# Chunk-selected attention and a gated MLP on one core: kmax left in PSUM until kmin is subtracted, with all queues reordered

## The chip, the cores and the metric

One Trainium2 chip, one NeuronCore. The time is device microseconds of a whole execution, the median of several runs; lower is better. One execution was also recorded by the hardware profiler, and all rows below come from it. TensorE is called PE there, VectorE DVE, ScalarE ACT, GpSimd POOL; SP is the engine that only issues DMAs here.

## The reference

Four batches of eight heads, 768 positions, head dimension 64. Keys come in chunks of 32. For every query and chunk an upper bound of the score is formed from the chunk's smallest and largest key per dimension; the six chunks with the highest bound are attended to. The result feeds a gated MLP block with a matrix multiply over positions.

```python
k_chunks = k.reshape(B, H, nc, 32, D)
k_min, k_max = k_chunks.min(axis=3), k_chunks.max(axis=3)
ub = sum_d maximum(q * k_min, q * k_max)          # [B, H, S, 24 chunks]
top = argsort(where(causal, ub, -1e9))[..., -6:]
scores = where(chunk of the key in top and causal, q @ k.T / 8, -1e9)
x = softmax(scores) @ v                            # laid out as [B, S, 512]
h = gelu(x @ w_in); u, v = split(h); v = layernorm(v) * g_ln
out = x + (u * (w_sg @ v + b_sg)) @ w_out
```

## The kernel before

The 32 heads are 16 pairs (p = 0 to 15), four to a batch. The upper bound is computed as q @ kmin + relu(q) @ (kmax - kmin), so that two small matmuls (`ub`) give it. The tile `W` holds kmin (its row 0) and kmax - kmin (its row 1) of a pair, 24 chunks each.

The program is a list of operations, each a function of an engine with what it reads and writes. `TABLE` holds the written-out order of each engine's queue as numbers of operations in that list, then the PSUM slot of every tile, and the engine of the operations that may run on one of several. Waits follow from reads and writes; an operation on a PSUM tile (`ps=`) also waits for every earlier operation of another engine on that tile, and the slot comes free when all of its operations are done. Engines work through their queues strictly in order. Operations are named here by tag:

- `kn`, `qn`, `vn`, `wi`, `ws`, `wo`: loads, issued by SP. `kT`, `dt_x`: DMA transposes. `st`: stores.
- `ktr`, `qtr` (TensorE, line 549): transposes of a pair's k and q, in halves hf of 384 columns, into PSUM.
- `kmm` (VectorE, line 579), pairs 0 to 7 (`kside`): minimum (m = 0) and maximum (m = 1) of the 12 chunks of one half, both from PSUM into `W` in SBUF. `wsub` (line 591): one subtraction per pair over 24 chunks, `W` row 1 minus row 0, all in SBUF, after all four `kmm`.
- `kev`, `qev`: evictions of the transposed halves to SBUF. `rel`: relu(q). `qcast`, `kcast`, `vcast`: casts to bf16.
- pairs 8 to 15: `kred` (line 598) reduces k as loaded, `perm` (line 620, `bounds`) puts the results in place by matmuls for two pairs at a time, in two tiles R; `wcp` (line 628) copies kmin and kmax of one tile to `W`, and `wsub` (line 633) subtracts 48 chunks of both pairs in SBUF, after both copies.
- `ub` (TensorE, lines 682 and 729), then `utr`, `m8`, `dn`, `dt` on VectorE select the chunks; `qd` puts the mask rows where the scores' matmuls read them; `mrow` fills the constant mask rows.
- `sc` (lines 838, 844 and 798) scores, `exp` (lines 853 and 804) on ScalarE, `aff` the causal cut on GpSimd, `pv` and `pvd` (lines 876, 883) the product with v, `rcp` and `xs` the division.
- the MLP of a batch: `hv`, `hu` (lines 930, 970) with `gv`, `gu` (gelu) on ScalarE; `bns`, `bna`, `var`, `rstd`, `nmr`, `vhat` the layer norm; `pt` (line 987), `vs`, `gt`, `ou` (line 1010), `os` (line 1016), `st`. `wic`, `wsc`, `woc`, `wst`, `wev` prepare the weights, `bev` the bias.

A batch's MLP runs between the attention of the next batch's pairs; the last batch's MLP has nothing beside it.

Of the kernel before, what the change touches and what calls it, by code (L numbers as in the profile page):

```python
# [1231 lines left out]
```

## Time and profile before

| | us |
|---|---|
| median of 3 runs (209.26 to 210.39) | 210.3 |
| the profiled execution | 211.3 |
| its span, first to last instruction | 209.6 |
| PE busy | 198.8 (95%) |
| DVE busy | 180.5 (86%) |
| ACT busy | 161.4 (77%) |
| POOL busy | 121.9 (58%) |

The busy time of PE holds pipelined matmuls whose ends are modelled, so it says where PE stood, not how near it is to its peak. A row of a timeline may stand for several instructions in sequence (x4); "idle before" is how long the engine had stood, and what ended it.

### The profile page before, as it was taken

Reading aid. Unit: us, or ns where it says so; the run is one execution under the profiler, and the core shown is the slowest. Engines: PE = TensorE matmul, PEld = TensorE weight load, DVE = VectorE, ACT = ScalarE, POOL = GpSimd, SP = SyncE. Lnnn points to the kernel's source line nnn. Section 1 sums busy time; section 2 is a strip of 40 time slices with the busy share of each in tenths; the row PEclk is TensorE's granted clock in tenths of the full one; section 3 lists DMA queues with packets and bytes.
Section 4 is the critical chain, followed back from the end, with each engine's and each line's share of the span. In section 5 each row is a group of like instructions: output and inputs, shape, how many; then the busy total and the mean of one; then the engine's idle time right before and its main releaser. Section 6 shows DMA issues by size and latency. Waiting matters only on the chain.

```text
span 209.6 us, 6043 instructions
## 1 busy us (share of the span) xinstructions
PE 198.8 (95%) x2392; PEld 129.0 (62%) x2392; DVE 180.5 (86%) x527; ACT 161.4 (77%) x238; POOL 121.9 (58%) x170
## 2 busy tenths in 40 slices
PE   5799999999999999999999999999899999899993
PEld 1655777755566677785456667677346767355652
DVE  3699899989999999999999899967868857587994
ACT  2559999997999899899788989888678887366000
POOL 8636799989579959958735957266580531002000
PEclk9999999999999999999999999999999999999999
DMA  6999999979949999999998995679968052401207
GB/s 143 221 252 208 227 243 316 298 206 276 222 126 255 238 146 252 192 182 153 218 218 154 217 206 125 133 146 117 200 122 191 4 91 42 149 0 50 100 32 272
DMA packets 103006, 36.38 MB, mean 174 GB/s; under 512 B 97729, under 2 KB 98497, under 8 KB 102978
## 3 DMA queue, kind: packets, MB, share of 16 engines
q1 hardware_dynamic: 102978, 36.00, 82.8%
q8 instruction: 19, 0.31, 0.7%
q14 instruction: 9, 0.07, 0.1%
HBM read 24.38 MB, written 6.29 MB: 146 GB/s over the span
## 4 chain that ended last, share of the span: by engine, by line
PE 61%; DVE 15%; ACT 8%; DMA 6%; SPq 3%; issue 3%; POOL 2%; DVEq 0%
PE PSG L987 11%; PE PSC L798 8%; PE PSG L970 8%; PE PSG L930 7%; PE PSG L1010 6%; PE PSG L876 5%; PE PSG L549 5%; ACT E L853 4%; PE PSG L729 3%; DMA vn<-in_v_dram 2%; DVE stats L939 2%; PE PSC L838 2%; DMA out_dram<-osb 2%; DVE osb L1016 2%; PE PSG L682 2%
## 5 line engine op out<-in xcount | busy, mean ns | idle before, releaser
L804 ACT ACTIVATE E<-PSC 128x1024 bf16<-128x1024 f32 (+1 forms) x72 | 62.6, 915 | 6.5 <-PE PSC L798 5.6
L798 PE MATMUL PSC<-QA,KA 128*128 128x128 bf16 (+2 forms) x336 | 37.6, 246 | 0.4 <-ACT E L804 0.4
L987 PE MATMUL PSG<-wsgT,vhat 128*128 128x384 bf16 x192 | 35.0, 326 | 0.0
L809 POOL TENSOR_SCALAR_AFFINE_SELECT E<-E 128x768 bf16<-128x768 bf16 x24 | 20.5, 863 | 24.0 <-ACT E L804 23.4
L798 PEld LDWEIGHTS PSC<-QA,KA 128*128 128x128 bf16 x336 | 24.2, 98 | 11.1 <-ACT E L804 3.8
L368 POOL CAST QA<-qT 64x768 bf16<-64x768 f32 (+1 forms) x27 | 22.2, 821 | 6.9 <-DVE qT L368 5.2
L975 ACT ACTIVATE uT<-PSG 128x384 bf16<-128x384 f32 x32 | 15.4, 486 | 12.1 <-PE PSG L970 11.8
L987 PEld LDWEIGHTS PSG<-wsgT,vhat 128*128 128x128 bf16 x192 | 17.9, 98 | 10.7 <-ACT vhat L953 0.4
L970 PE MATMUL PSG<-xT,winb 128*128 128x384 bf16 x128 | 23.8, 327 | 0.2 <-DVE U L738 0.2
L930 PE MATMUL PSG<-winb,xT 128*128 128x512 bf16 x96 | 22.2, 379 | 1.7 <-DVE PSG L993 0.9
L1010 PE MATMUL PSG<-woutb,uT 128*128 128x512 bf16 (+1 forms) x108 | 23.7, 355 | 0.0
L934 ACT ACTIVATE vgb<-PSG 128x512 f32<-128x512 f32 x24 | 14.3, 597 | 10.3 <-PE PSG L930 10.1
L993 DVE SCALAR_TENSOR_TENSOR PSG<-PSG,glnT,bsgbc 128x384 f32<-128x384 f32 x32 | 19.6, 614 | 2.9 <-PE PSG L987 2.4
L853 ACT ACTIVATE E<-PSC 128x1024 bf16<-128x1024 f32 (+1 forms) x24 | 20.6, 931 | 1.8 <-PE PSC L844 1.8
L368 POOL COPY QA<-Dt 32x576 bf16<-32x576 bf16 x20 | 13.8, 688 | 11.7 <-DVE Dt L757 10.6
L876 PE MATMUL PSG<-vx,E 128*128 128x65 bf16 x480 | 19.8, 194 | 0.4 <-ACT E L804 0.2
L579 DVE TENSOR_REDUCE Wall<-PSG 128x12 f32<-128x384 f32 x32 | 16.6, 543 | 3.4 <-PE PSG L549 3.4
L939 DVE BATCH_NORM_STATS2 stats<-vgb 128x6 f32<-128x512 f32 x24 | 16.1, 683 | 3.6 <-ACT vgb L934 3.3
L876 PEld LDWEIGHTS PSG<-vx,E 128*128 128x128 bf16 x480 | 17.1, 98 | 2.6 <-issue 0.6
L970 PEld LDWEIGHTS PSG<-xT,winb 128*128 128x128 bf16 x128 | 11.3, 98 | 11.2 <-ACT uT L975 3.0
L899 DVE TENSOR_TENSOR XS<-PSG,rden 128x384 bf16<-128x384 f32 x32 | 17.6, 551 | 0.7
L997 DVE TENSOR_TENSOR uT<-PSG,uT 128x384 bf16<-128x384 f32 x32 | 17.4, 550 | 0.6
(115 smaller groups left out, 377.0 us busy)
## 6 DMA issues: line engine op xcount, KB each, us to landing
vn<-in_v_dram SPq DMA_DIRECT2D x16, 384.0 KB, 5.5
qn<-in_q_dram SPq DMA_DIRECT2D x30, 192.0 KB, 4.5
out_dram<-osb SPq DMA_DIRECT2D x21, 256.0 KB, 2.5
kn<-in_k_dram SPq DMA_DIRECT2D x8, 384.0 KB, 6.3
kn<-in_k_dram SPq DMA_DIRECT2D x14, 192.0 KB, 4.6
uT<-in_moe_w_sg_dram SPq DMA_DIRECT2D x4, 384.0 KB, 5.4
vgb<-in_moe_w_in_dram SPq DMA_DIRECT2D x3, 512.0 KB, 7.5
vhat<-in_moe_w_sg_dram SPq DMA_DIRECT2D x2, 384.0 KB, 6.6
```

Of the source, the lines that this page charges most:

```text
L368: return e.tensor_copy(dst(), src())
L798: r = e.matmul(t.ap()[:, o:o + n], KA[w][i][:, 128 * kb:128 * kb + 128], QA[w][i][:, q0:q0 + n], start=True, stop=True)
L804: P.op("act", lambda e, t=t, c0=c0, c1=c1, i=i: e.activation(E[es][:, i, c0:c1], t.ap()[:, 0:c1 - c0], ACTF.Exp, scale=SCALE), act(c1 - c0 ...
L809: P.op("pool", lambda g, ev=ev: g.affine_select(ev, ev, pattern=[[0, NT], [1, 128]], compare_op=ALU.is_ge, fill=0.0, base=0, channel_multi ...
L853: P.op("act", lambda e, t=t, c0=c0, c1=c1, n=n: e.activation(E[es][:, :, c0:c1], t.ap().rearrange("p (i x) -> p i x", i=2)[:, :, 0:n], ACT ...
L876: r = e.matmul(t.ap()[:, 65 * qb:65 * qb + 65], E[es][:, i, a:a + 128], vx[w][:, kb, i, :], start=first, stop=False, skip_group_check=True)
L930: r = e.matmul(t.ap()[:, 0:F], xT[s][:, dk, 128 * qt:128 * qt + 128], winb[:, dk, F:DFF], start=(dk == 0), stop=(dk == NDK - 1))
L939: P.op("dve", lambda d, qt=qt, st=st: d.bn_stats(stats[st][:], vg[qt]), dve(F, 60), ("bns", b, qt), reads=[("vg", qt)], writes=[("stats", ...
L970: r = e.matmul(t.ap()[:, 0:TG], winb[:, dk, 128 * fb:128 * fb + 128], xT[s][:, dk, TG * tg:TG * tg + TG], start=(dk == 0), stop=(dk == NDK ...
L987: r = e.matmul(t.ap()[:, 0:TG], vhat[s][:, sb, 128 * fb:128 * fb + 128], wsgT[:, sb, TG * tg:TG * tg + TG], start=(sb == 0), stop=(sb == N ...
L993: P.op("dve", lambda d, t=t, fb=fb, tg=tg: d.scalar_tensor_tensor(t.ap()[:, 0:TG], t.ap()[:, 0:TG], glnT[:, fb:fb + 1], bsgbc[:, TG * tg:T ...
L1010: r = e.matmul(t.ap()[:, 0:c1 - c0], gT[s][:, fb, 128 * qt:128 * qt + 128], woutb[:, fb, c0:c1], start=(fb == 0), stop=(fb == NF - 1))
```

## The change

For pairs 0 to 7 the maximum of a half now goes to spare columns (384 to 395) of the PSUM tile that it was read from, and each half has a subtraction of its own right behind, 12 chunks wide, that reads kmax from PSUM and kmin from `W` and writes `W` row 1. For pairs 8 to 15 each tile R has a copy of kmin alone and a subtraction that reads kmax from PSUM. [...]

```diff
             c0, c1 = cols(hf, run)
+            n0, n1 = c0 // 32, c1 // 32
             for m, op in ((0, ALU.min), (1, ALU.max)):
-                P.op("dve", lambda d, m=m, op=op, t=t, c0=c0, c1=c1: d.tensor_reduce(
-                    W[w][:, m, c0 // 32:c1 // 32], t.ap()[:, 0:c1 - c0].rearrange("p (c x) -> p c x", x=32) if run == 0 else
...
-                    dve(c1 - c0), ("kmm", p, hf, m), reads=[t, ("W0", w)], writes=[("W", w, m, hf)], ps=[t])
+                P.op("dve", lambda d, m=m, op=op, t=t, c0=c0, c1=c1, n0=n0, n1=n1: d.tensor_reduce(
+                    W[w][:, 0, n0:n1] if m == 0 else t.ap()[:, TG:TG + n1 - n0],
+                    t.ap()[:, 0:c1 - c0].rearrange("p (c x) -> p c x", x=32), axis=AX.X, op=op),
+                    dve(c1 - c0), ("kmm", p, hf, m), reads=[t, ("W0", w)],
+                    writes=[("W", w, 0, hf) if m == 0 else ("Wm", w, hf)], ps=[t])
+            P.op("dve", lambda d, t=t, n0=n0, n1=n1: d.tensor_tensor(
+                W[w][:, 1, n0:n1], t.ap()[:, TG:TG + n1 - n0], W[w][:, 0, n0:n1], op=ALU.subtract), dve(12), ("wsub", p, hf),
+                reads=[("W", w, 0, hf), ("Wm", w, hf)], writes=[("W", w, 1, hf)], ps=[t])
...
-        ws = [("W", w, m, hf) for m in range(2) for hf in range(2)]
-        P.op("dve", lambda d: d.tensor_tensor(W[w][:, 1, 0:NC], W[w][:, 1, 0:NC], W[w][:, 0, 0:NC],
-                                              op=ALU.subtract), dve(24), ("wsub", p), port=True, reads=ws, writes=ws)
...
+        wv = lambda R, m: Wall[:, w0:w0 + 2, m, 0:NC].rearrange("p x (t R r) -> p x t R r", R=2, r=2)[:, :, :, R, :]
         for R in range(2):
-            P.op("dve", lambda d, R=R: d.tensor_copy(
-                Wall[:, w0:w0 + 2, :, 0:NC].rearrange("p x m (t R r) -> p (x m) t R r", R=2, r=2)[:, :, :, R, :], view(R)),
...
-        P.op("dve", lambda d: d.tensor_tensor(Wall[:, w0:w0 + 2, 1, 0:NC], Wall[:, w0:w0 + 2, 1, 0:NC],
-                                              Wall[:, w0:w0 + 2, 0, 0:NC], op=ALU.subtract), (125, 208),
-             ("wsub", pairs[0]), port=True, reads=ws, writes=ws)
+            P.op("dve", lambda d, R=R: d.tensor_copy(wv(R, 0), view(R)[:, 0::2]), dve(24),
+                 ("wcp", pairs[0], R), reads=[ts[R]] + [("W0", p % NW) for p in pairs],
+                 writes=[("W", p % NW, 0, R) for p in pairs], ps=[ts[R]])
+            P.op("dve", lambda d, R=R: d.tensor_tensor(wv(R, 1), view(R)[:, 1::2], wv(R, 0), op=ALU.subtract), dve(24),
+                 ("wsub", pairs[0], R), reads=[ts[R]] + [("W", p % NW, 0, R) for p in pairs],
+                 writes=[("W", p % NW, 1, R) for p in pairs], ps=[ts[R]])
```

All queues, all PSUM slots and the engine of some sixty operations are written anew in `TABLE`. The numbers in it shift, since there are 1304 operations where there were 1292. Read back into names, the stretches that matter below are:

```
VectorE, start   before  kmm_0_1_0 kev_0_1 kmm_0_1_1 . qev_0_0 qev_1_0 kmm_0_0_0 kmm_0_0_1 wsub_0 kmm_1_0_1 kmm_1_0_0 kmm_1_1_0 kmm_1_1_1 utr_0_0 wsub_1 m8_0_0
                 after   qev_1_1 qev_0_1 kmm_0_0_1 kmm_0_0_0 kmm_0_1_1 kmm_0_1_0 wsub_0_0 wsub_0_1 kmm_1_1_1 kmm_1_1_0 kmm_1_0_0 wsub_1_1 kmm_1_0_1 utr_0_0 wsub_1_0 m8_0_0
VectorE, 43 us   before  wev_0 qev_5_0 wsub_5 bns_0_1 wsub_4 rel_5 bns_0_0 bna_0_1 bns_0_3 bna_0_0 bna_0_3 utr_4_1
                 after   wev_0 bns_0_1 qev_6_1 bns_0_0 bna_0_1 bns_0_3 utr_4_1     (wsub_4_0 to wsub_5_0 stand earlier)
VectorE, 80 us   before  kred_11_0 wcp_8_0 os_0_1 wcp_8_1 rcp_5_0 kred_11_1 wsub_8 xs_5_0
                 after   wcp_8_1 wcp_8_0 gt_0_1_1 kred_11_0 os_0_2 os_0_1 wsub_8_0 wsub_8_1 kred_11_1 rcp_5_0
VectorE, end     before  os_3_2 os_3_0 os_3_3_256 os_3_3_0 os_3_1 and four halves
                 after   os_3_0 os_3_3_256 os_3_5_256 os_3_2 os_3_1 and four halves
SP, start        before  qn_1_0 kn_0_1_1 qn_1_1 kn_0_0_1 qn_0_0_0 qn_0_1_0 kn_0_0_0 kn_0_1_0 kn_1_0 qn_0_1_1 qn_0_0_1 kn_1_1
                 after   qn_1_1 kn_0_1_0 qn_1_0 qn_0_1_1 kn_0_1_1 qn_0_0_1 qn_0_0_0 kn_0_0_1 kn_0_0_0 qn_0_1_0 kn_1_1 kn_1_0
SP, weights      before  vn_2 wi_3 vn_3 wi_2 qn_5_0 wi_1 wi_0 ws_0 ws_2
                 after   vn_2 ws_0 qn_5_0 vn_3 wi_0 wi_2 wi_1 wi_3 qn_6_1 qn_6_0 ws_2
SP, 110 us       before  kT_11_0 kT_11_1 qn_15_1 kT_12_1 kn_15 vn_11 qn_15_0 vn_9 st_0_5 vn_10
                 after   kT_10_1 qn_15_1 vn_8 vn_9 kn_14 vn_10 kn_15 qn_15_0 kT_11_0
```

Operations that change engine: from VectorE to ScalarE kev_0_1, kev_4_0_0, kev_4_1_1, qev_0_0, qev_1_0, qev_2_1, qev_3_0, qev_4_1, qev_5_0, qev_12_1, qev_14_1, rel_5, wev_5, xs_4_1 (six instructions there), vhat_0_5, vhat_2_3, vhat_3_1, vhat_3_4; from ScalarE to VectorE qev_0_1, qev_1_1, qev_3_1, qev_6_1, qev_11_1, qev_12_0, kev_2_0, kev_3_1, kev_5_0_0, xev_0_0, both bev, vhat_3_2, vhat_3_5; from GpSimd to ScalarE qcast_0, qcast_1, wic_1, mrow_3_0_0, kcast_8_1, kcast_10_0, both kcast_12, kcast_15_0, woc_0, woc_3, qd_7_0, qd_9_1, qd_11_0, rel_8, vcast_11; from ScalarE to GpSimd ini_0, rel_1, rel_3, rel_7, rel_10, wsc_0, wsc_4, both qd_6, qd_12_0, kcast_10_1, kcast_11_1, kcast_14_1, vcast_7, vcast_9, vcast_12, vcast_15, qcast_13_0.

## Rows read from the trace of the kernel before

**Rows 1.** Stretches: length, then busy us (instructions) of PE, PEld, DVE, ACT, POOL; clock, DMA.

```profile
15.00:39.00 24.00, 23.58 (x461) 17.39 (x461) 22.53 (x81) 23.15 (x32) 19.86 (x25) 1.00 1.09 257
39.00:62.40 23.40, 22.92 (x224) 14.47 (x221) 22.14 (x67) 21.89 (x40) 18.83 (x26) 1.00 0.90 214
62.40:98.50 36.10, 35.79 (x555) 25.63 (x553) 35.15 (x104) 33.85 (x50) 29.45 (x41) 1.00 1.17 205
...
112.00:130.00 18.00, 17.48 (x286) 12.15 (x285) 16.46 (x41) 16.39 (x22) 14.71 (x19) 1.00 1.05 184
130.00:148.00 18.00, 17.12 (x262) 12.30 (x261) 14.90 (x59) 16.02 (x19) 9.70 (x14) 1.00 0.80 137
148.00:180.00 32.00, 31.07 (x311) 18.66 (x311) 24.13 (x57) 23.60 (x33) 11.54 (x16) 1.00 0.53 118
```

**Rows 2.** Lines 591, 633 and 628: count, duration ns min/median/max, first and last start.

```profile
L591 DVE TENSOR_TENSOR Wall<-Wall x8: 138/194/717, 10.4 to 64.5; 128x24 f32<-128x24 f32 x8
L633 DVE TENSOR_TENSOR Wall<-Wall x4: 172/198/778, 83.0 to 130.4; 128x48 f32<-128x48 f32 x4
L628 DVE COPY Wall<-PSG x8: 169/200/210, 81.2 to 125.7; 128x48 f32<-128x48 f32 x8
```

**Rows 3.** Timeline at two subtractions: start us, us, engine, line; idle before.

```profile
45.02 0.83 POOL L368 COPY KA<-INDF 64x768 bf16<-64x768 bf16 x1
45.16 0.72 DVE L591 TENSOR_TENSOR Wall<-Wall 128x24 f32<-128x24 f32 x1
82.91 0.82 POOL L368 CAST QA<-qT 64x768 bf16<-64x768 f32 x1
83.02 0.78 DVE L633 TENSOR_TENSOR Wall<-Wall 128x48 f32<-128x48 f32 x1
83.85 0.72 PE L729 MATMUL PSG<-qT,Wall 64*32 64x288 f32 x16 [0.31 <-DVE Wall L633]
```

**Rows 4.** Groups by line and shape on VectorE: busy us, mean ns; idle before.

```profile
L579 DVE TENSOR_REDUCE Wall<-PSG 128x12 f32<-128x384 f32 x32 | 16.6, 543 | 3.4 <-PE PSG L549 3.4
L993 DVE SCALAR_TENSOR_TENSOR PSG<-PSG,glnT,bsgbc 128x384 f32<-128x384 f32 x32 | 19.6, 614 | 2.9 <-PE PSG L987 2.4
L997 DVE TENSOR_TENSOR uT<-PSG,uT 128x384 bf16<-128x384 f32 x32 | 17.4, 550 | 0.6
```

**Rows 5.** Groups by line and shape on ScalarE and GpSimd.

```profile
L365 ACT ACTIVATE qT<-PSG 128x384 f32<-128x384 f32 x23 | 11.0, 496 | 2.3 <-PE PSG L549 2.1
L365 ACT ACTIVATE rT<-qT 128x576 f32<-128x576 f32 x9 | 6.0, 681 | 0.1
L365 ACT ACTIVATE vx<-vn 128x768 bf16<-128x768 f32 x5 | 4.2, 847 | 0.8 <-DMA vn<-in_v_dram 0.8
L423 ACT ACTIVATE CMw<-CMw 64x32 bf16<-64x32 bf16 x1 | 0.2, 228 | 3.4 <-POOL CMw L416 3.4
L367 POOL TENSOR_SCALAR rT<-qT 128x576 f32<-128x576 f32 x5 | 8.2, 1650 | 0.8 <-ACT qT L365 0.7
```

**Rows 6.** Timeline of ScalarE and TensorE near 123 us.

```profile
122.64 0.85 ACT L365 ACTIVATE vx<-vn 128x768 bf16<-128x768 f32 x1 [0.78 <-DMA vn<-in_v_dram]
124.46 0.62 PE L798 MATMUL PSC<-QA,KA 128*128 128x128 bf16 x7 [0.36 <-ACT E L804]
```

**Rows 7.** Timeline of VectorE at the start.

```profile
10.75 1.95 DVE L579 TENSOR_REDUCE Wall<-PSG 128x12 f32<-128x384 f32 x4 [0.17 <-PE PSG L549]
```

**Rows 8.** Chain of waits (first row) and VectorE's timeline at the end.

```profile
201.20 3.48 PE PSG L1010 x20
204.70 0.69 DVE L1016 TENSOR_TENSOR osb<-PSG,XS 128x512 f32<-128x512 f32 x1 [0.36 <-PE PSG L1010]
205.31 1.56 DVE L1016 TENSOR_TENSOR qn<-PSG,XS 128x256 f32<-128x256 f32 x4
```

**Rows 9.** Timeline of GpSimd and TensorE near 40 us.

```profile
39.09 3.00 POOL L368 CAST winb<-vgb 128x1024 bf16<-128x1024 f32 x3
42.73 1.04 PE L930 MATMUL PSG<-winb,xT 128*128 128x512 bf16 x4
```

More of the change, by code (lines that the diff above doesn't have):

```diff
@@ L577, in kside @@
             c0, c1 = cols(hf, run)
+            n0, n1 = c0 // 32, c1 // 32
             for m, op in ((0, ALU.min), (1, ALU.max)):
-                P.op("dve", lambda d, m=m, op=op, t=t, c0=c0, c1=c1: d.tensor_reduce(
-                    W[w][:, m, c0 // 32:c1 // 32], t.ap()[:, 0:c1 - c0].rearrange("p (c x) -> p c x", x=32) if run == 0 else
-                    t.ap()[:, 0:c1 - c0].rearrange("p (e c x) -> p c e x", e=2, x=16), axis=AX.X if run == 0 else AX.XY, op=op),
-                    dve(c1 - c0), ("kmm", p, hf, m), reads=[t, ("W0", w)], writes=[("W", w, m, hf)], ps=[t])
+                P.op("dve", lambda d, m=m, op=op, t=t, c0=c0, c1=c1, n0=n0, n1=n1: d.tensor_reduce(
[6 more added lines that the diff above has]
+                reads=[("W", w, 0, hf), ("Wm", w, hf)], writes=[("W", w, 1, hf)], ps=[t])
         for hf, t in enumerate(ts):
@@ L626, in bounds @@
              reads=["identF"] + [("Bn", u, x, m) for x in range(2) for m in range(2)], writes=ts, alloc=tuple(ts))
+        wv = lambda R, m: Wall[:, w0:w0 + 2, m, 0:NC].rearrange("p x (t R r) -> p x t R r", R=2, r=2)[:, :, :, R, :]
         for R in range(2):
-            P.op("dve", lambda d, R=R: d.tensor_copy(
-                Wall[:, w0:w0 + 2, :, 0:NC].rearrange("p x m (t R r) -> p (x m) t R r", R=2, r=2)[:, :, :, R, :], view(R)),
-                (125, 208), ("wcp", pairs[0], R), reads=[ts[R]] + [("W0", p % NW) for p in pairs],
-                writes=[("W", p % NW, m, R) for p in pairs for m in range(2)], ps=[ts[R]])
-        ws = [("W", p % NW, m, hf) for p in pairs for m in range(2) for hf in range(2)]
-        P.op("dve", lambda d: d.tensor_tensor(Wall[:, w0:w0 + 2, 1, 0:NC], Wall[:, w0:w0 + 2, 1, 0:NC],
-                                              Wall[:, w0:w0 + 2, 0, 0:NC], op=ALU.subtract), (125, 208),
-             ("wsub", pairs[0]), port=True, reads=ws, writes=ws)
+            P.op("dve", lambda d, R=R: d.tensor_copy(wv(R, 0), view(R)[:, 0::2]), dve(24),
[4 more added lines that the diff above has]
+                 writes=[("W", p % NW, 1, R) for p in pairs], ps=[ts[R]])
     def qside(p):
@@ L1103 @@
     "pe": (
[14 rows of a table removed]
-    "act": (
[9 rows of a table removed]
-    "dve": (
[16 rows of a table removed]
-    "pool": (
[13 rows of a table removed]
[14 rows of a table added]
+    "act": (
[9 rows of a table added]
+    "dve": (
[16 rows of a table added]
+    "pool": (
[13 rows of a table added]
     "slots": (
-        "1003113221103233010010110113201100023103200110102313231200101012201000010101230110011233333232223223333"
-        "3222322322101101221000001132010101110011330101001023100101322323323232322233233332332201101032011011012"
-        "2011010001101231000110023010110323223322233233223322232233211001032010101330001113310101032113100001113"
-        "01213001002321322013"),
+        "1310230210323012101010013202300110132013111010102302322010011013210101001011231010010232323323223333222"
+        "3323323223100111230000001123111010110101230011000132100110323232323323223322233223223310011023001010102"
+        "3010110001010320110100132100101232332233322322232232323333311010023010011320010013201111023102130210231"
+        "02113211100203320213"),
     "engine": (
[8 rows of a table removed]
[8 rows of a table added]
 }
```

118 rows, old and new, of the table TABLE are left out of this document.

## The prediction

> **What bounds the kernel now.** I read the view by stretches first. From 15 us on no engine has room: TensorE is busy 23.58 of 24.00 us, then 22.92 of 23.40, then 35.79 of 36.10, and even later it idles only 0.52, 0.88 and 0.93 us in a stretch; VectorE stands at 93 to 97% up to 98.5 us and ScalarE at 94 to 96% [rows 1]. The reader is to see in these rows that TensorE ends the kernel from about 39 us, that before this the exponentials of the first four pairs on ScalarE do (23.15 of 24.00 us), and how little can be won: from 39 to 180 us TensorE's idle time is 0.48 + 0.31 + 0.52 + 0.88 + 0.93 = 3.12 us. Then I went to the lines that are edited, and to the places where TensorE or ScalarE stands.
>
> **The subtraction itself.** In the kernel before, kmax minus kmin takes both operands from SBUF. It lasts 138 ns at best, 194 in the median, but 717 at worst (line 591), and 172, 198 and 778 (line 633) [rows 2]. The long ones end with a GpSimd instruction: the one that starts at 45.16 us runs 0.72 us, to 45.88, and GpSimd's copy of 45.02 runs to 45.85; the one of 83.02 runs to 83.80, GpSimd's cast of 82.91 to 83.73 [rows 3]. So a subtraction of two SBUF operands is held while GpSimd reads. The copies of line 628, which read PSUM, are not: 169 to 210 ns, eight times [rows 2]. A subtraction with kmax in PSUM should then cost what line 628 costs. Bounds of one: 0.14 us (best of line 591) and 0.21 (longest of line 628); I take 0.17 for 12 columns, near line 628, whose source it shares.
>
> Sum on VectorE: 20 instructions (8 and 4 subtractions, 8 copies) at the medians of [rows 2] are 4.0 us, and the two longest holds add 0.52 and 0.58: at least 5.1. They become 32 (16 subtractions for pairs 0 to 7, then 8 copies of half the columns and 8 subtractions), 32 x 0.17 = 5.4 us. The load doesn't change by what counts; what goes is the holds. The 16 kmax results are now written to PSUM: a reduction of 384 columns takes 543 ns, and the nearest pair of rows for a PSUM against an SBUF output is 614 against 550 ns [rows 4], so between nothing and 16 x 0.064 = 1.0 us; a gain is excluded, since the columns read set the time. I take nothing, as only 12 columns are written.
>
> [...]
>
> **New waits.** An operation on a PSUM tile waits for earlier ones of other engines on it. kev, where it runs on ScalarE, so waits for its half's wsub too, and what is queued behind it on ScalarE (qcast_0, the next kev and qev) waits along; scores wait for those. One wsub, 0.17 us, is the price; it hides as long as ScalarE waits before the first exponential anyway. The tile's slot is also freed one wsub later. In bounds the wait gets shorter: ub waits for two short instructions that GpSimd can't hold.
>
> **Where TensorE gets time back.**
> (1) ub_8: TensorE idles 0.31 us before 83.85 for the held subtraction [rows 3]. Now both halves stand ahead of kred_11_1 and can't be held: -0.31.
> (2) 43 to 49 us: two subtractions stand among bns_0_1, rel_5 and ub_4; the one of 45.16 is held 0.53 us over the median [rows 2, 3]. Both now stand earlier, and rel_5 moves to ScalarE. TensorE's idle time of the stretch is 0.48 us [rows 1]; bounds -0.48 and 0, I take -0.30.
> (3) Exponentials of pairs 0 to 3. Between the first and the last of them kev_2_0, kev_3_1 and rel_3 leave ScalarE (0.50 + 0.50 + 0.68 us) and one qev and two kev come (3 x 0.50, all of 384 columns) [rows 5]: -0.18. rel_3 costs GpSimd 1.65 us [rows 5]; it has 24.00 - 19.86 = 4.1 us free there [rows 1].
> (4) vn_9: its cast waits on ScalarE for the load 0.78 us, the next exponential is late, and TensorE idles 0.36 us at 124.46 [rows 6]. SP now issues vn_9 right after vn_8, ahead of kn_14, and the cast is on GpSimd: -0.36 (bounds -0.36 and 0).
>
> **Where it loses.**
> (5) Start: pair 1's four reductions run from 10.75 us and the transpose of pair 0's scores follows them [rows 7]; wsub_1_1 now stands among the four: +0.17. All four reductions of pair 0 now come after its last loads, two more than before: at worst 2 x 0.54 = 1.1 us [rows 4]. I take nothing for it: pair 1's last key load keeps the twelfth place in SP's queue, and the reductions of 10.75 wait for that.
> (6) End: os_3_2 now stands behind os_3_5_256, right before os_3_1. Rows of the end give 0.69 us for a full and 1.56 / 4 = 0.39 us for a half [rows 8]: 1.08 us of VectorE behind ou_3_5_256, while the matmuls of ou_3_1 take some 0.86 (2048 columns, where 8192 take 3.48 us): +0.24.
> (7) ws_0 (384 KB) now goes ahead of the four loads of w_in. The last cast of w_in ended at 42.1 us, TensorE's first use came at 42.73 [rows 9]. The bounds are nothing and 1.5 us (384 KB at the 257 GB/s of the stretch before [rows 1]). That first use also needs the last transposed block of x, which comes after the last exponential, and one of the four casts is on ScalarE now, so I take nothing; if that cover is gone, up to 0.9 us comes in, the 1.5 less the 0.6 from the last cast to the first use.
>
> Sum: -0.31 - 0.30 - 0.18 - 0.36 + 0.17 + 0.24 = -0.74 us. The profiled execution took 211.3 us (209.6 of span and 1.7 around), 0.5% over the median of 210.3; 211.3 - 0.7 = 210.6, and in the same ratio **209.6 us** on the median.
>
> **Rivals.**
> A, the order closes more. TensorE shows 3.12 us of idle from 39 to 180 us [rows 1]; all queues are new, and two thirds of it would be -2.1: 209.2 in the profile, 208.2 us. For it: VectorE loses its longest holds, and from 130 us on no engine but TensorE is near full. Against it: I find no other wait that the new order clearly removes.
> B, slower: ScalarE becomes the bound from 62.4 to 98.5 us. There it gains kcast_8_1, kcast_10_0, two woc, rel_8, qd_7_0, qd_9_1 and xs_4_1, and loses rel_7, rel_10, both qd_6, kcast_10_1, vcast_7 and qev_11_1. By [rows 5]: 2 x 0.50 + 2 x 0.62 (between the rows for 384 and 768 columns) + 3 x 0.68 + 6 x 0.23 = 5.7 in, 4 x 0.68 + 0.50 + 0.85 + 0.50 = 4.6 out, +1.1 us against 36.10 - 33.85 = 2.25 us idle [rows 1]. It decides when the idle time is not to be had, because ScalarE stands there for scores that TensorE can't give sooner. Then 1.1 us comes in, (1) to (4) are lost behind it, and start and end stay: 211.3 + 1.1 + 0.17 + 0.24 = 212.8, or 211.8 us on the median.
> C, the step doesn't do what it says: PSUM operands are dearer than I take them, 16 + 24 instructions by 0.064 us [rows 4], 2.6 us, of which half would lie on the path: 211.3 - 0.7 + 1.3 = 211.9, or 210.9 us.
>
> **How the numbers follow.** This kernel's runs tell about 0.5% (1.05 us) from no change; the line for "faster" is 209.25 us, close below my forecast. Chances: my sum 0.38 (its own range 208.8 to 210.5: 0.26 within 0.5%, 0.12 faster), A 0.30 (faster), B 0.24 (slower), C 0.08 (0.06 within, 0.02 slower). Faster 0.42, within 0.32, slower 0.26. The range leaves out a tenth on either side, the far ends of A and B (B with part of the 1.1 us of (5)): 207.8 to 212.0.
>
> **What would show it.** Right: no subtraction over 0.25 us in the profile of the changed kernel, no wait of TensorE for the subtraction of pairs 8 and 9, first exponential at 15.6 to 15.9 us, first gelu at 43.5 to 44.5, a last store as late after ou_3_1 as now. Step (4): no wait of a vx cast for its load near 122 us. A: idle of TensorE from 112 to 180 us under 1.2 us. B: ScalarE busy over 34.7 of the 36 us before the second batch's gelu, and TensorE's idle there over 1 us. C: subtractions or the kmax reductions longer by 60 ns. I am wrong if the first exponential comes a microsecond later, or if a load (w_in, vn, kT) ends a wait of TensorE where none does now.

## The result, and the profile after

The changed kernel takes 212.75 us (median of four runs, 212.18 to 213.94), the kernel before, beside it, 209.78: a ratio of 1.0125, 95% interval 1.0081 to 1.0169. It is slower by 1.2%; a second measurement (e6 below) gave 1.0119 [1.0056, 1.0183]. The profiled execution took 213.94 us, its span is 211.8 (before: 211.3 and 209.6). Executions of one program lie up to 5.5 us apart in this case (the kernel before, beside e17: 208.59 to 214.10 us), and the ratios leave out those that are over 1.5% above the fastest of their kernel; of e15 three of twelve are left out so, the profiled one among them.

The stretches of the changed kernel, to be laid beside [rows 1] (length, then busy us (instructions) of PE, PEld, DVE, ACT, POOL; clock, DMA):

```profile
39.00:62.40 23.40, 22.68 (x250) 14.88 (x249) 20.80 (x67) 22.09 (x38) 19.91 (x28) 1.00 1.03 241
62.40:98.50 36.10, 35.26 (x521) 25.91 (x524) 34.85 (x109) 34.98 (x58) 32.47 (x43) 1.00 0.98 184
98.50:112.00 13.50, 12.00 (x95) 6.09 (x95) 12.87 (x45) 10.21 (x19) 6.97 (x9) 1.00 0.98 199
112.00:130.00 18.00, 18.00 (x274) 12.22 (x273) 15.87 (x36) 17.07 (x25) 13.55 (x16) 1.00 1.12 207
130.00:148.00 18.00, 16.14 (x236) 11.72 (x239) 13.62 (x45) 13.62 (x18) 11.09 (x15) 1.00 0.86 169
148.00:180.00 32.00, 31.53 (x347) 19.93 (x350) 25.46 (x72) 26.72 (x36) 13.13 (x17) 1.00 0.40 88
```

The stretch from 98.5 to 112 us of the kernel before, which [rows 1] leaves out:

```profile
98.50:112.00 13.50, 13.46 (x81) 6.97 (x82) 12.83 (x46) 11.23 (x20) 6.82 (x8) 1.00 0.98 191
```

The reader is to see TensorE's idle time move. It fell from 112 to 130 us (0.52 to none) and from 148 to 180 (0.93 to 0.47), and rose from 0.04 to 1.50 us from 98.5 to 112 and from 0.88 to 1.86 from 130 to 148. From 39 to 180 us it was 3.16 us in all before and is 5.39 now. The last two stretches each hold one wait. The first, in the timeline (start us, us, engine, line; idle before and what ended it):

```profile
105.27 1.26 SPq L607 DMA_TRANSPOSE KA<-kbx  x1
108.39 0.49 ACT L976 ACTIVATE uT<-PSG 128x384 bf16<-128x384 f32 x1 [0.16 <-PE PSG L971]
110.39 0.94 ACT L365 ACTIVATE kbx<-kn 128x384 bf16<-128x384 f32 x2 [1.51 <-DMA KA<-kbx]
111.23 0.47 ACT L976 ACTIVATE uT<-PSG 128x384 bf16<-128x384 f32 x1
111.76 0.82 PE L971 MATMUL PSG<-xT,winb 128*128 128x384 bf16 x4 [1.45 <-ACT uT L976]
```

Read upward. TensorE waits 1.45 us for a gelu of batch 1 (line 976). That gelu stands behind two casts of pair 12's keys, `kcast_12_1` and `kcast_12_0`, which the change moved from GpSimd to ScalarE. They write `kbx`, which is free when the transposing load `kT_10_1` has read it; SP issued that at 105.27, and the casts begin at 110.39, 5.1 us later.

The second wait, SP's stores and loads among the rest:

```profile
133.52 1.29 SPq L607 DMA_TRANSPOSE KA<-IND  x1
134.85 1.29 SPq L908 DMA_TRANSPOSE xT<-XS  x1
135.00 0.69 DVE L1017 TENSOR_TENSOR osb<-PSG,XS 128x512 f32<-128x512 f32 x1
136.19 0.58 SPq L1024 DMA_DIRECT2D out_dram<-osb  x1
...
136.81 1.26 SPq L607 DMA_TRANSPOSE KA<-kbx  x1
...
138.12 0.57 SPq L1024 DMA_DIRECT2D out_dram<-osb  x1
...
142.02 1.29 DVE L1017 TENSOR_TENSOR osb<-PSG,XS 128x512 f32<-128x512 f32 x2 [2.13 <-DMA out_dram<-osb]
142.76 0.64 PE L877 MATMUL PSG<-vx,E 128*128 128x65 bf16 x15 [1.74 <-DVE osb L1017]
```

The output rows `os_1_0` are ready at 135.69. Their store goes out at 138.12, since SP first ends one transposing load, then issues the store of `os_1_2` and one more transposing load, `kT_14_1` (0.6 and 1.3 us). Only three buffers `osb` exist; `os_1_3` needs the one of that store, VectorE stands 2.13 us for it, and the product with v of pair 10 (line 877) waits for the PSUM that `os_1_3` and `os_1_5` free: 1.74 us. The chain of waits goes straight through this store (start us, us, what):

```profile
138.12 3.81 DMA out_dram<-osb
...
142.02 0.70 DVE osb L1017
...
142.76 0.64 PE PSG L877 x15
```

The edit itself did what was forecast of it. Lines 580 (the reductions; the row with output PSG is kmax), 585 and 634 (the subtractions), count and ns min/median/max:

```profile
L580 DVE TENSOR_REDUCE PSG<-PSG x16: 525/555/567, 8.7 to 67.2; 128x12 f32<-128x384 f32 x16
L580 DVE TENSOR_REDUCE Wall<-PSG x16: 511/546/556, 9.2 to 66.2; 128x12 f32<-128x384 f32 x16
L585 DVE TENSOR_TENSOR Wall<-PSG,Wall x16: 129/157/171, 10.9 to 68.1; 128x12 f32<-128x12 f32 x16
L634 DVE TENSOR_TENSOR Wall<-PSG,Wall x8: 132/170/178, 84.2 to 128.3; 128x24 f32<-128x24 f32 x8
```

No subtraction is held any more: 178 ns at most, where [rows 2] had 717 and 778.

The start is later as well. The first half of the first block scores on TensorE and the first exponential, before and after:

```profile
11.04 0.69 PE L682 MATMUL PSG<-qT,Wall 64*32 64x288 f32 x8
11.53 0.69 PE L682 MATMUL PSG<-rT,Wall 64*32 64x288 f32 x8
15.59 3.78 ACT L853 ACTIVATE E<-PSC 128x1024 bf16<-128x1024 f32 x4 [1.54 <-PE PSC L844]
```

```profile
11.91 1.19 PE L683 MATMUL PSG<-qT,Wall 64*32 64x288 f32 x8
12.87 1.18 PE L683 MATMUL PSG<-rT,Wall 64*32 64x288 f32 x8
17.36 1.94 ACT L854 ACTIVATE E<-PSC 128x1024 bf16<-128x1024 f32 x2 [1.30 <-PE PSC L845]
```

The first exponential is 1.77 us late, and the same eight matmuls take 1.19 us against 0.69. From the start of these eight to the start of the next eight it is 0.96 us against 0.49, twice as long. The start shows TensorE at two levels: up to 8.4 us in the profile before, and up to 11.6 us here, the transposes of line 549 mostly follow one another at 213 ns within a run of them; from 9.3 and from 14.4 us on at 109. (The clock column reads 1.00 here in both profiles, so the level is read from the matmuls; the first record of a granted clock begins at 8.39 us in the trace before and at 14.18 us in this one.) So there were two suspects, **the start** and **the two waits**, and the question whether the code or the order is to blame.

### The profile page after: what moved, and what is told of

The parts are those of the page before. It is cut to its first block, busy times and chain, and to the rows that moved or that the text cites. A ratio compares the mean times of both kernels' runs of the same rounds, so it can differ in the third digit from the quotient of the medians.

```text
span 211.8 us, 6047 instructions
## 1 busy us (share of the span) xinstructions
PE 199.3 (94%) x2375; PEld 130.5 (62%) x2392; DVE 179.5 (85%) x535; ACT 162.8 (77%) x245; POOL 126.8 (60%) x172
## 4 chain that ended last, share of the span: by engine, by line
PE 67%; ACT 12%; DVE 7%; SPq 5%; DMA 5%; issue 2%; DVEq 0%
PE PSG L988 14%; PE PSC L799 12%; ACT E L854 7%; PE PSG L1011 7%; PE PSG L971 7%; PE PSG L931 7%; PE PSG L549 6%; PE PSG L877 5%; PE PSG L730 3%; DMA KA<-kbx 2%; PE PSG L683 2%; PE PSG L884 2%; DMA out_dram<-osb 2%; SPq L512 2%; SPq L519 2%
## 5 line engine op out<-in xcount | busy, mean ns | idle before, releaser
L810 POOL TENSOR_SCALAR_AFFINE_SELECT E<-E 128x768 bf16<-128x768 bf16 x24 | 21.0, 882 | 19.5 <-ACT E L805 18.9
L988 PEld LDWEIGHTS PSG<-wsgT,vhat 128*128 128x128 bf16 x192 | 17.6, 98 | 11.6 <-DVE uT L998 0.6
L368 POOL CAST QA<-qT 64x768 bf16<-64x768 f32 (+1 forms) x26 | 21.5, 825 | 2.5 <-PE PSC L799 1.5
L1011 PE MATMUL PSG<-woutb,uT 128*128 128x512 bf16 (+1 forms) x96 | 21.3, 352 | 0.7 <-DVE PSG L994 0.2
L931 PE MATMUL PSG<-winb,xT 128*128 128x512 bf16 x91 | 21.2, 379 | 0.5 <-issue 0.3
L877 PEld LDWEIGHTS PSG<-vx,E 128*128 128x128 bf16 x480 | 17.2, 98 | 3.7 <-DVE osb L1017 2.3
L368 POOL COPY QA<-Dt 32x576 bf16<-32x576 bf16 x20 | 13.3, 664 | 10.3 <-DVE Dt L758 8.4
L900 DVE TENSOR_TENSOR XS<-PSG,rden 128x384 bf16<-128x384 f32 x31 | 16.9, 551 | 0.7
L549 PE MATMUL PSG<-identF,qn 128*128 128x128 f32 x96 | 16.6, 298 | 0.7 <-DMA qn<-in_q_dram 0.7
```

Source lines behind the costliest of these rows:

```text
L368: return e.tensor_copy(dst(), src())
L549: r = e.matmul(t.ap()[:, 128 * j:128 * j + 128], src[:].rearrange("p i t d -> p (i t d)")[:, 128 * x:128 * x + 128], identF[:], is_transpo ...
L810: P.op("pool", lambda g, ev=ev: g.affine_select(ev, ev, pattern=[[0, NT], [1, 128]], compare_op=ALU.is_ge, fill=0.0, base=0, channel_multi ...
L877: r = e.matmul(t.ap()[:, 65 * qb:65 * qb + 65], E[es][:, i, a:a + 128], vx[w][:, kb, i, :], start=first, stop=False, skip_group_check=True)
L931: r = e.matmul(t.ap()[:, 0:F], xT[s][:, dk, 128 * qt:128 * qt + 128], winb[:, dk, F:DFF], start=(dk == 0), stop=(dk == NDK - 1))
L988: r = e.matmul(t.ap()[:, 0:TG], vhat[s][:, sb, 128 * fb:128 * fb + 128], wsgT[:, sb, TG * tg:TG * tg + TG], start=(sb == 0), stop=(sb == N ...
```

## The experiments

All ratios are to the kernel before, run beside each kernel, with the 95% interval.

| kernel | ratio |
|---|---|
| changed kernel, twice | 1.0125 [1.0081, 1.0169], 1.0119 [1.0056, 1.0183] |
| e1 new code, old order | 1.0062 [1.0020, 1.0104] |
| e2 old code, new order | 1.0227 [1.0166, 1.0289] |
| e3 changed, nine warm-up matmuls | 1.0094 [1.0061, 1.0127] |
| e4 changed, old start | 1.0061 [1.0032, 1.0090] |
| e7 both waits mended (casts on ScalarE) | 1.0044 [1.0012, 1.0076] |
| e8, e17 before, nine warm-ups | 0.9985 [0.9948, 1.0022], 0.9996 [0.9958, 1.0034] |
| e9 old order, new code for pairs 8 to 15 | 1.0015 [0.9982, 1.0049] |
| e10 old order, new code for pairs 2 to 15 | 1.0038 [1.0000, 1.0075] |
| e11 both waits mended (casts on GpSimd) | 1.0066 [1.0028, 1.0104] |
| e12 as e11, nine warm-ups | 1.0022 [0.9985, 1.0059] |
| e13 as e11, old start | 1.0039 [1.0010, 1.0068] |
| e14 as e13, old code for pairs 0 and 1 | 1.0044 [1.0007, 1.0081] |
| e15 changed, one load moved on SP | 1.0026 [0.9990, 1.0062] |
| e18 as e9, nine warm-ups | 1.0015 [0.9978, 1.0053] |

### Code or order: e1 and e2

e1 is the changed code with the old `TABLE`; each new subtraction stands right behind its pair of reductions, or its copy. e2 is the old code with the new `TABLE`; the one subtraction stands where the later of its halves stood.

```diff
 # VectorE's queue at the start, by names: e1
-kmm_0_1_0 kev_0_1 kmm_0_1_1 init_14 ... kmm_0_0_0 kmm_0_0_1 wsub_0
+kmm_0_1_0 kev_0_1 kmm_0_1_1 wsub_0_1 init_14 ... kmm_0_0_0 kmm_0_0_1 wsub_0_0
-kmm_1_0_1 kmm_1_0_0 kmm_1_1_0 kmm_1_1_1 utr_0_0 wsub_1
+kmm_1_0_1 kmm_1_0_0 wsub_1_0 kmm_1_1_0 kmm_1_1_1 wsub_1_1 utr_0_0
```

> The new code (kmax left in PSUM, one subtraction per half) with the queues, engines and slots of the kernel before. [...] Rival 'the code costs it' (PSUM operands, twice as many subtractions on VectorE, more waits): 211 us or more, with the first exponential a microsecond or more late.

> The new order of all queues with the old code (kmax evicted to SBUF, one subtraction per pair, placed where the later of the two halves stood; for the pairs of blocks behind both copies). Theory 'the order costs it': TensorE's first matmuls stand as in the changed kernel, the first exponential comes at 17.0 to 17.9 us, and the time is 212.2 to 213.6 us. Rival 'the code costs it': the first exponential within 0.5 us of 15.6 us and 209.5 to 210.5 us.

Both theories, 'the order costs it' and 'the code costs it', were too simple. e1 came to 1.006 and not level with the kernel before: its median of 211.04 us is at the edge of the rival's, but its first exponential, at 16.13 us, is half a microsecond late and not a whole one. e2 came to 1.023, worse than the changed kernel and than its own theory. In e2 the old subtractions stand beside other GpSimd work than before; its lines 591 and 633, and the place where it hurts:

```profile
L591 DVE TENSOR_TENSOR Wall<-Wall x8: 139/286/1620, 11.1 to 69.3; 128x24 f32<-128x24 f32 x8
L633 DVE TENSOR_TENSOR Wall<-Wall x4: 465/778/1049, 85.7 to 130.7; 128x48 f32<-128x48 f32 x4
```

```profile
41.40 1.03 POOL L368 CAST winb<-vgb 128x1024 bf16<-128x1024 f32 x1
41.82 1.62 DVE L591 TENSOR_TENSOR Wall<-Wall 128x24 f32<-128x24 f32 x1
42.38 1.03 POOL L368 CAST winb<-xT 128x1024 bf16<-128x1024 f32 x1
43.97 0.55 PE L549 MATMUL PSG<-identF,qn 128*128 128x128 f32 x3 [1.42 <-DVE XS L899]
```

One subtraction of 24 columns is held from 41.82 to 43.44, until two casts of GpSimd are over, and TensorE then stands 1.42 us for the work behind it on VectorE. In the kernel before, too, the four longest (0.38, 0.72, 0.44 and 0.78 us, at 43.72, 45.16, 64.55 and 83.02) each end 0.03 to 0.06 us behind a copy or cast of GpSimd (line 368). The prediction's "while GpSimd reads" is too wide for its trace: the subtraction of 19.59 us took 184 ns inside a relu of GpSimd (line 367, 18.44 to 20.09). With kmax in PSUM, 13 of the changed kernel's 24 subtractions begin while a copy or cast of line 368 runs, and they take 130 to 178 ns. So the code is worth about 1% in the new order, which leans on it (with the one subtraction put at the place of the later half; the two intervals just touch), and it costs 0.6% in the old one. Why the missing holds gain nothing there is not shown.

### What of the code costs in the old order: e9, e10, e18

```diff
 # kside of the changed kernel (e9: n = 8, e10: n = 2); old order
-                    W[w][:, 0, n0:n1] if m == 0 else t.ap()[:, TG:TG + n1 - n0],
+                    W[w][:, m, n0:n1] if m == 0 or p < n else t.ap()[:, TG:TG + n1 - n0],
...
+        if p < n:
+            P.op("dve", lambda d: d.tensor_tensor(W[w][:, 1, 0:NC], W[w][:, 1, 0:NC], W[w][:, 0, 0:NC],
+                                                  op=ALU.subtract), dve(24), ("wsub", p), port=True, reads=ws, writes=ws)
```

(`port=True`, here and in the diff of the change, is a note in the list of operations that changes no instruction.)

> The old order with the new code for the pairs whose bounds are copied by blocks (8 to 15) alone; pairs 0 to 7 keep kmax in SBUF and one subtraction each. The new code throughout, in the old order, came to 1.006 of the kernel before. Theory 'the halves of pairs 0 to 7 cost it': 0.997 to 1.003, and the start is as in the kernel before (the transpose of the first scores on VectorE follows the last reduction of pair 1 within 0.1 us). Rival 'the blocks' bounds cost it, or the order no longer fits': 1.004 to 1.009.

> The old order with the new code for pairs 2 to 15; pairs 0 and 1 alone keep kmax in SBUF and one subtraction each, which come before the first exponential. Theory 'the start costs it' (two subtractions ahead of the first transposed scores on VectorE, each behind the end of a reduction that wrote PSUM, and PSUM tiles held for them): 0.997 to 1.003, first exponential 0.3 to 0.6 us earlier than with the new code throughout at the same point of TensorE's clock. Rival 'the subtractions in the stage up to 40 us or those of the blocks cost it': 1.004 to 1.009.

> The old order, the new code for the blocks' bounds of pairs 8 to 15 alone, and nine warm-up matmuls: the part of the change that was level with the kernel before (1.0015), with the start that gave 0.9985. Theory 'both are worth little': 0.997 to 1.001. Rival 'they add to a gain': under 0.997.

e9 is within its theory; e10, at 1.0038, lies between its theory and its rival. The medians fall in the order that the theory wants (1.006, 1.004, 1.0015), but the intervals overlap, so a share for each part is not shown. What is shown is the place. VectorE in e1, before the transpose of the first scores (line 693):

```profile
11.93 0.17 DVE L585 TENSOR_TENSOR Wall<-PSG,Wall 128x12 f32<-128x12 f32 x1
...
13.07 0.17 DVE L585 TENSOR_TENSOR Wall<-PSG,Wall 128x12 f32<-128x12 f32 x1
13.15 0.47 DVE L693 STREAM_TRANSPOSE U<-PSG 128x288 f32<-128x288 f32 x1
```

The four reductions of pair 1 begin at 10.87 there, so the transpose follows 2.28 us later. In the kernel before they begin at 10.75 [rows 7] and the transpose at 12.62, 1.87 later, and in e10, with the old code for these two pairs, 13.06 - 11.19 = 1.87. Two subtractions ahead of the first scores cost 0.41 us, 0.2 each. The warm-ups of e18 add no gain to e9 (1.0015 both).

### The start: e3, e4, e8, e17

```diff
 # e3 (changed kernel), e8 and e17 (kernel before)
-    NWARM = 6
+    NWARM = 9
 # e4: SP's first 12 loads and all queues up to ub_0 as before; SP shown
-qn_1_1 kn_0_1_0 qn_1_0 qn_0_1_1 kn_0_1_1 qn_0_0_1 qn_0_0_0 kn_0_0_1 kn_0_0_0 qn_0_1_0 kn_1_1 kn_1_0
+qn_1_0 kn_0_1_1 qn_1_1 kn_0_0_1 qn_0_0_0 qn_0_1_0 kn_0_0_0 kn_0_1_0 kn_1_0 qn_0_1_1 qn_0_0_1 kn_1_1
```

> The changed kernel with nine warm-up matmuls of 128x512 on TensorE in place of six, and nothing else changed: 1.4 us more of matmuls at their 0.46 us, so that TensorE has no gap from the warm-up to 7.1 us. Theory 'TensorE's clock at the start': the transposes come 109 ns apart before 8 us already, the 18 matmuls of the first block scores take 1.3 to 1.4 us in place of 2.31, the first exponential is at 15.5 to 16.2 us, and the time falls by 1.2 to 2.0 us to 210.7 to 211.6 us. Rival 'loads and evictions set the start': the first exponential stays at 17.2 us or later, and the time is 212.3 to 213.5 us.

> The changed kernel with the start of the kernel before: the first 12 loads on SP, and each engine's queue up to the first block scores of pair 0, in the old order and on the old engines (the subtractions per half as in the new code); all behind it as in the changed kernel. Theory 'the start is two thirds of the loss': first exponential at 15.5 to 16.0 us, TensorE's transposes 109 ns apart from 8.4 us on, and 210.6 to 211.5 us. Rival 'the start is given back later' (what comes early waits at the 110 and 141 us stalls, whose ends a transfer sets): first exponential as early, but 212.0 us or more.

> The kernel before with nine warm-up matmuls in place of six. Theory 'the clock at the start is worth time in both kernels': transposes 109 ns apart from 5 to 6 us on, first exponential at 15.2 to 15.5 us, and 0.3 to 0.8 us less than the kernel before. Rival 'loads set the start of the kernel before': the same transposes faster, but the first exponential at 15.5 us or later and the time within 0.3 us of 210.0 us.

> The kernel before with nine warm-up matmuls once more, since three rounds gave 0.9985 [0.9948, 1.0022]. Theory 'an earlier rise of TensorE's clock saves a little in the old order too': 0.996 to 0.999. Rival 'nothing': 0.999 to 1.002.

In e3 the first exponential came at 16.17 us, 1.2 us earlier, as the theory said, but the time fell by 0.3% in place of 0.6 to 0.9, within the intervals of no change. In e4 the time fell by half of the loss, yet its profile shows the start no earlier: first exponential 17.28 us, the eight matmuls 1.19 us, though the queues were the old ones. Here the clock column shows a fall: TensorE ran at the higher level first (three transposes in 0.55 us at 5.80, where the changed kernel takes 0.90 at 7.76), then the granted clock is 0.51 for 3.5 us:

```profile
10.70:14.20 3.50, 3.50 (x25) 1.61 (x24) 2.57 (x7) 1.98 (x4) 1.71 (x3) 0.51 1.32 219
```

Ahead of the fall TensorE had waited three times, 0.81, 0.78 and 0.39 us. e1, with the start of the kernel before as well, waited as long at the same places (0.81, 0.79, 0.39) and kept 1.00 in the same stretch. In the kernel before, nine warm-ups are worth nothing that can be measured (0.9985 and 0.9996). So the start was not what I took it for; that called for second profiles of the two kernels themselves.

### Two more profiles: e5 and e6

> The kernel before once more, unchanged, for a second profiled execution. If the point at which TensorE's matmuls go from 213 to 109 ns apart belongs to the order of the queues, it is 8.4 us again, the first block scores begin at 11.0 us and the first exponential at 15.6 us. If it differs between executions of one program (the old order with the new code had it at 4.6 us, with the same loads), it is another one, and the first exponential moves by 0.3 us or less, since only transposes ahead of a load that lands later run slower.

> The changed kernel once more, unchanged: a second profiled execution and a closer time. [...] Rival 'that execution was unlucky': the 18 matmuls take 1.3 us, the first exponential comes at 16.2 to 16.6 us, and the time is 211.5 to 212.2 us.

e5, the kernel before:

```profile
11.70 1.19 PE L682 MATMUL PSG<-qT,Wall 64*32 64x288 f32 x8
17.08 1.94 ACT L853 ACTIVATE E<-PSC 128x1024 bf16<-128x1024 f32 x2 [1.31 <-PE PSC L844]
```

e6, the changed kernel:

```profile
11.20 0.69 PE L683 MATMUL PSG<-qT,Wall 64*32 64x288 f32 x8
15.92 2.86 ACT L854 ACTIVATE E<-PSC 128x1024 bf16<-128x1024 f32 x3 [1.66 <-PE PSC L845]
```

The roles are swapped: now the kernel before has the late start and the changed kernel the early one. The first exponential of the kernel before moved by 1.5 us, where at most 0.3 was expected; and in e6 the rival's early start came without the rival's time, since its median is 213.56 us. The level of TensorE's clock at the start differs between executions of one program (0.69 and 1.19 us for the same eight matmuls, in either kernel); it belongs to neither order. At equal level the new start is late by 17.36 - 17.08 = 0.28 and 15.92 - 15.59 = 0.33 us. In the two executions of the kernel before the matmuls go to the faster spacing near 8.4 and near 14 us. And in the two profiles of the kernel before the late start costs nothing: e5 ends at 208.5 us, earlier than the 209.6 of the first. In e6 the wait at 110 us is gone, the one behind it isn't (waits of PE from 100 us on: us in total, times, longest; then three stretches):

```profile
PE PSG L877 <- DVE osb L1017: 2.1, 1, 2.1
```

```profile
138.00:142.00 4.00, 1.92 (x34) 1.34 (x32) 1.29 (x2) 1.78 (x3) 3.14 (x5) 1.00 0.90 228
142.00:145.50 3.50, 3.50 (x55) 3.26 (x52) 2.18 (x7) 1.73 (x2) 0.41 (x1) 0.52 0.43 109
145.50:148.00 2.50, 2.50 (x47) 1.38 (x45) 1.37 (x3) 1.66 (x3) 2.31 (x4) 0.99 0.78 58
```

The wait for the store is paid twice here: TensorE stands 2.1 us, and behind that the granted clock is 0.52 for 3.5 us. The new theory: the loss is the waits, above all the one for the store. Its rival: the waits take the place of others that come later anyway.

### The waits: e7, e15, e11, e16

```diff
 # SP's queue (e7, e11 to e16)
-kT_13_0 dt_x_2_1 st_1_2 kT_14_1 st_1_0 vn_15 st_1_1 st_1_3
+kT_13_0 dt_x_2_1 st_1_2 st_1_0 vn_15 st_1_1 kT_14_1 st_1_3
 # ScalarE's queue (e7)
-gu_1_3_0 kcast_12_1 kcast_12_0 gu_1_1_0 ... gu_1_0_1 gu_1_0_0
+gu_1_3_0 gu_1_1_0 ... gu_1_0_1 gu_1_0_0 kcast_12_1 kcast_12_0
 # GpSimd's queue (e11 to e14, e16; not on ScalarE there)
-kcast_11_0 rstd_1 qd_10_0
+kcast_11_0 rstd_1 kcast_12_1 kcast_12_0 qd_10_0
```

> The changed kernel with three steps moved: ScalarE's two casts of pair 12's keys go behind the last gelu of sequence 1, where TensorE's 1.6 us wait at 110 us came from; and SP issues pair 14's transposing load behind the two output stores that it stood ahead of, where the 1.9 us wait at 141 us came from. Theory 'both stalls are on the path to the end': the first is gone, the second is under 1.0 us, and the time falls by 1.5 to 2.5 us to 210.2 to 211.4 us. Rival 'the stalls took the place of waits that come later anyway' (the changed kernel was 3.9 us behind at 116 us and 4.4 at 145, but only 2.2 behind at the end): the waits are gone or moved, and the time stays within 0.7 us, at 211.9 to 213.0 us.

> The changed kernel with one DMA moved on SP and nothing else: pair 14's transposing load goes behind the two output stores of sequence 1. Theory 'the wait of 1.7 to 2.1 us at 139 to 142 us is the loss of the new order behind its start': 1.004 to 1.008, and the wait on the store is under 0.8 us. Rival 'the wait at 110 us matters too' (it was there in one of two profiled executions of the changed kernel): 1.008 to 1.011.

> The changed kernel with SP's order mended as before (pair 14's transposing load behind the two output stores), and the two casts of pair 12's keys back on GpSimd, right behind the reciprocal root of sequence 1, where GpSimd is idle, in place of ScalarE. With them behind the gelus on ScalarE the wait at 110 us was gone, but the first exponentials of pair 8 came behind them and TensorE waited 0.7 us at 115 us. Theory 'the rest of the loss is that wait and the start': 209.9 to 210.9 us, no wait over 0.5 us between 108 and 118 us. Rival 'the new order loses elsewhere': 211.0 to 211.7 us.

> One more look at the changed kernel with pair 12's casts on GpSimd and the store mended. [...]

e7 fell to 1.0044, 0.8% below the changed kernel: about two thirds of the loss, just within its theory's range (211.36 us) and against the rival. Its waits of PE from 100 us on:

```profile
PE PSC L799 <- ACT E L805: 0.7, 1, 0.7
PE PSG L931 <- DMA xT<-XS: 0.6, 1, 0.6
```

Both waits are gone; the 0.7 us is the edit's own, exponentials of pair 8 that now stand behind the casts. One moved load (e15) does as much by its time, 1.0026. Its one profile, of an execution of 214.49 us, doesn't show how: it had the late start (first exponential 16.86 us, the eight matmuls 1.18), and with it both waits:

```profile
PE PSG L971 <- ACT uT L976: 2.0, 1, 2.0
PE PSG L877 <- DVE osb L1017: 1.4, 1, 1.4
```

The store waits there behind two other transposing loads:

```profile
135.84 0.69 DVE L1017 TENSOR_TENSOR osb<-PSG,XS 128x512 f32<-128x512 f32 x1
136.27 1.29 SPq L908 DMA_TRANSPOSE xT<-XS  x1
137.61 1.05 SPq L1024 DMA_DIRECT2D out_dram<-osb  x2
```

The rows of `os_1_0` are ready at 136.53, and SP begins with the two stores at 137.61. VectorE then stands 1.85 us for the buffer and TensorE 1.4, where under 0.8 us was expected. So in the changed kernel's profiles `kT_14_1` stands ahead of the late store, but it is not the only way to this wait.

The late start seems to tie the two suspects together. With the early start (e6) SP issues `kT_10_1` at 103.75 us and the casts run at 108.09 without a wait; in the changed kernel's first profile it is issued at 105.27, lands 5.1 us later, and ScalarE comes to the casts at 108.9, before the load is in. Of four profiled new orders with the casts on ScalarE and a late start (the changed kernel, e2, e15, e4) three have this wait, 1.4 to 2.0 us, and neither of the two with an early start (e6, e3) has it. In e4 the load was issued at 104.94 and was in when ScalarE came, 4.2 us later; why it took longer in the other three is not shown. So a late start can cost time in the new order that it didn't cost in e5, but six profiles are too few to call it shown.

With the casts on GpSimd (e11, e16) no wait over 0.5 us is left behind 100 us, but the time is no better than e7's: the theory missed, 211.67 us where 209.9 to 210.9 was expected, and the rival's 211.0 to 211.7 holds. e16's one execution took 210.28 us, near the lower end of e11's twelve (209.6 to 213.6), so what the upper ones do stays open.

### Do the two add up: e12, e13, e14

e12 is e11 with nine warm-ups, e13 e11 with e4's start, e14 e13 with the old code for pairs 0 and 1.

> The same with nine warm-up matmuls in place of six. Theory 'the level of TensorE's clock at the start is worth little, since what starts early waits later': within 0.4 us of the same kernel with six. Rival 'it is worth its time': 0.8 us or more below it, 209.0 to 210.0 us.

> The changed kernel with both places mended at once: the start of the kernel before (each queue up to the first block scores of pair 0, new subtractions), pair 12's casts on GpSimd, and pair 14's transposing load behind the two stores. The old start alone was 1.0061 of the kernel before, the two stalls mended alone 1.0044 (casts on ScalarE) and 1.0066 (on GpSimd), the changed kernel 1.012. Theory 'two losses that add': 0.997 to 1.002. Rival 'each only hides the other' (the end is set elsewhere, by what both leave): 1.004 to 1.008.

> The same with the old code for pairs 0 and 1 as well (kmax in SBUF, one subtraction each, in their old places): the start is then wholly that of the kernel before, and what is left of the change is the new code from pair 2 on and the new order behind the start, mended. In the old order the new code cost 0.6% throughout and 0.4% from pair 2 on. Theory 'the start's subtractions cost 0.2%': 0.001 to 0.004 below the same kernel with new subtractions. Rival 'no difference': within 0.001 of it. If the forecast's gains behind the start (the held subtractions, 43 to 49 us, the last block) are real, this comes to 0.994 to 0.998.

The nine warm-ups took 0.4% off e11 by the medians, the rival's size and not the theory's, but the intervals overlap. The two mends don't add up: e13 is 1.0039 and e14 1.0044, where e11 alone is 1.0066 and the sum would be 1.000. With the waits mended, the old start gives 0.3%, inside the intervals; perhaps what it gave in e4 was largely the wait at 110 us, which e4's profile doesn't have. e14 takes away the start's subtractions too, and is not faster than e13, against its theory. It was also to be 0.994 to 0.998 if the forecast's gains behind the start were real: they don't show in the time. No version beats the kernel before, and the rest, some 0.4%, isn't settled. Two parts of it show in rows: 0.3 us at the start, and 0.2 at the end (below).

## Why the prediction was wrong

The forecast was 209.6 us, range 207.8 to 212.0; 212.75 lies above it. By its own steps:

**The subtraction itself, right.** 0.17 us from PSUM was forecast; 157 and 170 ns came, and no hold. The kmax reductions into PSUM were taken at nothing; they cost 9 ns each by the medians (555 against 546), 0.15 us in all, where the bound was 1.0. Rival C falls: 24 columns took 170 ns in the median with kmax in PSUM, and 194 with both operands in SBUF [rows 2].

**New waits, right.** `kev_0_0` on ScalarE stands 0.57 us until the two subtractions of 10.92 us are over, and the first block scores on TensorE wait 0.33 for the tile that it frees. It is of the size of the 0.3 us of (5); whether it is the same 0.3 us is not shown.

**(1) right; (4) right in mechanism, sized from one execution.** No wait of TensorE for the subtraction of pairs 8 and 9 is left in e6 or the changed kernel; the kernel before has it again in e5 (0.32 us). The cast of `vn_9` runs on GpSimd at 122.31 us, and TensorE stands nowhere from 112 to 130 us. But in e5 it stood only 0.09 us there, and ScalarE's cast 0.18 us in place of 0.78: most of the 0.36 belonged to the first profile and not to the kernel.

**(2) and (3), gain not there.** From 39 to 62.4 us TensorE idles 0.72 us, and 0.44 in e6, against 0.48 [rows 1] and 0.15 in e5: nothing for the forecast 0.30. The holds of VectorE are gone from this stretch, and TensorE's idle time didn't fall with them. From the start of the first exponential of pairs 0 to 3 to the start of the last it is 23.1 us in both kernels (17.4 to 40.4, and 15.6 to 38.7), and 23.4 in e6 (15.9 to 39.3), not 0.18 less. The gains (1), (2) and (4) were taken from the 3.12 us of idle time that the first profile shows from 39 to 180 us (3.16 with the stretch left out); in e5 the same kernel has 1.12 us there.

**(5) Start, right in size, wrong in kind.** +0.17 was forecast, 0.3 measured at equal clock; a subtraction ahead of the first scores costs 0.2 (e1, e10). I read one profile's start as the kernel's: the first exponential at 15.6 us was that execution's, and 17.1 in the next.

**(6) End, right.** +0.24 was forecast (its own terms, 1.08 less 0.86, give 0.22). From the first matmul of the last batch's second product to the end of the span it is 17.0 us in e5 (191.48 to 208.5) and 17.2 after (194.63 to 211.8).

**(7) `ws_0`, right.** The last cast of `w_in` ends 0.6 us ahead of TensorE's first use in e6 as before, and no wait of TensorE for it shows.

**The failing step is a term that the sum didn't have: new waits on the path.** I followed the operations that the edit and the named moves touch, and for the rest wrote "I find no other wait that the new order clearly removes". I didn't ask which waits it adds. The prediction's rule for being wrong, "if a load (w_in, vn, kT) ends a wait of TensorE where none does now", came true twice through other engines: `kT_10_1` by way of a cast on ScalarE, and `kT_14_1` by way of a store that stood behind it on SP. Both could have been read from the queues: two casts moved from GpSimd to ScalarE, in among the gelus that TensorE waits for, with a target that a transposing load sets free; and two stores, of a ring of three buffers, that now have `kT_14_1` between them. The price of the second was there as well: a transposing load took SP 1.29 us to issue in the kernel before (line 605: the median, and the one of 137.10 us). In the changed kernel's profile these two waits cost TensorE 1.45 and 1.74 us, where the whole sum was -0.74; mending both takes off 0.8% in e7 and 0.6% in e11, and what makes the rest of the loss stays open.

**Rival B, right in size, wrong in mechanism.** ScalarE's load from 62.4 to 98.5 us rose by 1.13 us, as forecast (33.85 to 34.98, where +1.1 was worked out), the first of its two signs. The second, over 1 us of idle on TensorE, didn't come (0.84 us against 0.31 before, and 0.48 in e6), so ScalarE didn't become the bound there; that its 211.8 us lies nearest to the result is luck. **Rival A** had half its condition (no idle from 112 to 130) and lost it between 130 and 148.

## What to carry to other kernels

When all queues are new, list for each engine what now stands ahead of the instructions that the bounding engine waits for, and for each of those what frees its target: a cast into a buffer that a load still reads, or a store behind loads on one issuing queue, is a wait on the bounding engine at one remove (here 1.45 and 1.74 us). An edit and an order are one design: the same new code cost 0.6% in the old order and saved 1% in the new one. And a start or an idle time read from one profile is that execution's (first exponential of the kernel before: 15.59 and 17.08 us); take a second profile before it goes into a sum.
